# Two decode layers on one core: MLP columns in another order, ninth rows whole on even and odd partitions, and a shorter end of GELU

## The chip, the cores and the metric

The kernel runs on one core of one Trainium2 chip. The metric is the device time of one execution in microseconds (us). All data are 32-bit floats. The core has a matrix engine (TensorE, PE in the profile; its weight loads are PEld), a vector engine (VectorE, DVE), a scalar engine (ScalarE, ACT), GpSimd (POOL) and a queue engine SP that here only issues transfers (DMAs) from device memory (HBM) into the on-chip memory SBUF. SBUF has 128 partitions. TensorE writes its sums into PSUM.

## The reference

There are two sequences (B = 2) with one new position each. One layer is an attention over a cache of 8,192 keys and values per head, 32 heads of 128, and then a gated MLP of width 4,608. The same weights and caches are used in both layers.

```python
def _B_ref(x, w_gate, w_up, w_down):          # the MLP
    g = jnp.einsum("bsd,df->bsf", x, w_gate)   # 576 -> 4608
    u = jnp.einsum("bsd,df->bsf", x, w_up)
    h = _gelu(g) * u                           # tanh form of GELU
    return jnp.einsum("bsf,fd->bsd", h, w_down)

x = A_x
x = x + _A_ref(_layernorm(x), A_k_cache, A_v_cache, A_wq, A_wo)
x = x + _B_ref(_layernorm(x), B_w_gate, B_w_up, B_w_down)
x = x + _A_ref(_layernorm(x), A_k_cache, A_v_cache, A_wq, A_wo)
x = x + _B_ref(_layernorm(x), B_w_gate, B_w_up, B_w_down)
```

## The kernel before

The kernel is written out by hand as `attention(0)`, `mlp(0)`, `attention(1)`, `mlp(1)`. The second attention goes through the heads in reverse order, so that some keys and values that the first left in SBUF are used again.

**Space and the order of transfers.** All weights and caches go through one SBUF tile, `space`, of 50,176 words per partition. A list, `queue`, holds the loads in the order in which they are to be issued. Each time the program has used a piece, `done(key)` frees its words and `pump()` takes as many loads off the list as find room. `Arena` decides where they go: `ring` gives the first layer's MLP pieces four places of 2,304 words by turns; `fit`, used in the second layer's MLP, looks for a free stretch, first behind the last piece given, then from word 0, then behind each live piece. All loads are issued on SP, one after another; an issue waits until the last reader of its words is done. The waits of SP in the trace also show that an issue waits for the landing of the transfer that stands eight places before it.

**Gate and up, first layer** (`split_rows`, `split_middle`, `split_products`). The 4,608 columns are done in two halves h. For one half and one of the two weights, the 576 rows are seen as 64 groups of 9 neighbouring rows. `split_rows` loads rows 2u and 2u+1 of each group (u = 0 to 3) onto the even and the odd partitions, 64 runs of 2,304 words each. The ninth rows of gate and of up share one piece, `split_middle`. Before, the even partitions held the first quarter of columns of the half and the odd ones the second, and beside each other in the partition lay gate and up: eight transfers over both halves of columns. `split_products` multiplies each piece as soon as it has landed: two sides k, four groups c of 288 columns on four quarters of the array (L1097). A filler product (`idle_products`, L586) follows each piece; its result isn't used.

**Gate and up, second layer** (`all_products`, L1113). Pieces are whole: 5, 4 row groups of gate, then 3, 3, 2, 1 of up (`GU[1]`).

**Activation** (`activate`, L1119 to L1135). For each half v: ScalarE multiplies by 1/sigma (L1122), VectorE transposes 32x32 blocks (L1124), and 36 values per partition go through the tanh form of GELU: VectorE (L1127 to L1129), tanh on ScalarE (L1130), VectorE (L1131, L1132), and the result times 0.5 is written twice into `hT`, by VectorE (L1134) and by ScalarE (L1135).

**Down** (`down`, `DOWN`, L1150). `hT` is the stationary operand with 4 columns. Each row of w_down that a partition holds costs 8 matmul instructions of 144 columns (4 column groups, two instructions each). The rows were seen as 4 blocks t of 128 partitions with 9 neighbouring rows each. The first layer took them in pieces of 4 rows, and the four ninth rows as one last piece (two transfers). The second layer took three whole blocks (9 rows, 2,592 KB) and the fourth in pieces of 3, 3, 2, 1 rows. `IDLE` says how much filler stands ahead of each piece. `add_to_x` (L579) adds the sum to x; at the very end x is stored from SP and from ScalarE.

Of the kernel before, what the change touches and what calls it, by code (L numbers as in the profile page):

```python
# [9 lines left out]
F32 = mybir.dt.float32  # L10
AF = mybir.ActivationFunctionType
ALU = mybir.AluOpType
# [3 lines left out]
P = 128  # L16
B = 2
# [3 lines left out]
D = 576  # L21
DF = 4608
# [6 lines left out]
NU = 9  # L29
EQ = 512  # L30
HG = DF // 16
PAD = 6
NT = 4
NI = DF // (NT * P)
# [90 lines left out]
def decode_layers(ctx, tc, x_in, kc, vc, wq, wo, wg, wu, wd, out):  # L125
    nc = tc.nc
# [4 lines left out]
    once = ctx.enter_context(tc.tile_pool(name="once", bufs=1))  # L131
# [7 lines left out]
    for c in range(4):  # L139
        for s in range(2):  # L140
            lo = 32 * c + s * B
# [6 lines left out]
    queue, ready, places = [], {}, {}  # L148

    def pump():  # L150
        while queue and queue[0]():
            queue.pop(0)

    def done(key):
        arena.free(key)
        pump()

    def part_at(at, n):
        return space[:, at:at + n]
# [78 lines left out]
    def weights(key, n, first, transfers):  # L238

        def make():  # L240
            at = arena.ring(key, n) if first is None else arena.fit(key, n, first)
            if at is None:
                return False
            t = ready[key] = part_at(at, n)
            transfers(t)
            return True

        queue.append(make)
# [22 lines left out]
    def split_rows(name, w, h, u):  # L271

        rows = w[:, DF // 2 * h:DF // 2 * (h + 1)].rearrange("(m r) w -> m r w", r=NU)

        def transfers(t):
            for e in range(2):
                nc.sync.dma_start(t[e::2, :], rows[:, 2 * u + e, :])

        weights((name, 0, h, u), DF // 2, None, transfers)

    def split_middle(h):

        def transfers(t):
            for g, w in enumerate((wg, wu)):
                for e in range(2):
                    lo, n = DF // 4 * (2 * h + e), DF // 4
                    nc.sync.dma_start(
                        t[e::2, n * g:n * (g + 1)], w[:, lo:lo + n].rearrange("(m r) w -> m r w", r=NU)[:, NU - 1, :]
                    )

        weights(("gu", 0, h), DF // 2, None, transfers)

    def down(layer, rows):

        (t0, i0), (t1, i1) = rows[0], rows[-1]
        src = wd.rearrange("(t p i) c -> p t i c", t=NT, i=NI)[:, t0:t1 + 1, i0:i1 + 1, :]

        def transfers(t):
            if t0 == t1:
                nc.sync.dma_start(t.rearrange("p (i c) -> p i c", c=D), src[:, 0])  # L300
            else:
                to = t.rearrange("p (t c) -> p t c", c=D)
                for lo, hi in ((0, 3), (3, NT)):
                    nc.sync.dma_start(to[:, lo:hi, :], src[:, lo:hi, 0, :])

        weights(("d", layer, rows[0]), len(rows) * D, whole_at[layer], transfers)

    def products():

# [9 lines left out]
    def out_rows(layer, g):  # L319
# [13 lines left out]
    GU = [[range(0, 5), range(5, NU)], [range(0, 3), range(3, 6), range(6, 8), single[-1]]]  # L333

    DOWN = [
        [[(t, i) for i in range(lo, lo + 4)] for t in range(NT) for lo in (0, 4)] + [[(t, NI - 1) for t in range(NT)]],
        [[(t, i) for i in range(NI)] for t in range(NT - 1)]
        + [[(NT - 1, i) for i in range(lo, hi)] for lo, hi in ((0, 3), (3, 6), (6, 8), (8, 9))],
    ]

    IDLE = [(2, 2, 2, 2, 2, 2, 2, 2, 1), (4, 4, 4, 1)]

    whole_at = (None, 0)
    def groups(layer):
# [76 lines left out]
    def plan_mlp(layer):  # L421
        if layer == 0:
            for h in range(2):
                for u in range(4):
                    split_rows("g", wg, h, u)
                split_middle(h)
                for u in range(4):
                    split_rows("u", wu, h, u)
        else:
            for g, (name, w) in enumerate((("g", wg), ("u", wu))):  # L430
                for us in GU[g]:
                    half_rows((name, layer, us[0]), w, us, 0)
        for rows in DOWN[layer]:
            down(layer, rows)

    plan_first()
    plan_mlp(0)
# [62 lines left out]
    acc = psum1.tile([P, 2, 512], F32, name="acc")  # L500
# [5 lines left out]
    xps = bank[:, 0:CW]  # L506
# [71 lines left out]
    def add_to_x():  # L578
        nc.vector.tensor_add(x, xps, x)  # L579
# [497 lines left out]
    def mlp(layer):  # L1077
        split = layer == 0
        rstd = norm(split)
        if split:  # L1080
            idle_products(2, 1)
        hT = once.tile([P, 2, NI, 2, 2, B], F32, name="hT", tag="xc")

        def window(u, at):

            return xt[:, PAD + 32 * u - at:PAD + 32 * u - at + 4 * B]

        def split_products(h):

            steps = [(("g", layer, h, u), u, 2, (0,)) for u in range(4)] + [(("gu", layer, h), 4, 1, (0, 1))]  # L1090
            steps += [(("u", layer, h, u), u, 2, (1,)) for u in range(4)]
            for key, u, sides, gs in steps:
                w = ready.pop(key).rearrange("p (k c w) -> p k c w", c=4, w=HG)
                for k in range(2):
                    g, e = (k, 0) if u == 4 else (gs[0], k)
                    for c in range(4):
                        nc.tensor.matmul(  # L1097
                            acc[32 * c:32 * c + 4 * B, h, :HG], window(u, 4 * g + 2 * e), w[:, k, c, :],
                            start=(key == steps[0][0] and k == 0), stop=(key == steps[-1][0] and k == 1),
                        )  # L1100
                done(key)
                if key != steps[-1][0]:
                    idle_products(1, None if h else 1)

        def all_products():

            for g, name in enumerate("gu"):
                for us in GU[g]:
                    w = ready.pop((name, layer, us[0])).rearrange("p (u v c w) -> p u v c w", v=2, c=4, w=HG)
                    for u in us:  # L1110
                        for v in range(2):
                            for c in range(4):
                                nc.tensor.matmul(  # L1113
                                    acc[32 * c:32 * c + 4 * B, v, :HG], window(u, 4 * g), w[:, u - us[0], v, c, :],
                                    start=(g == 0 and u == 0), stop=(g == 1 and u == NU - 1),
                                )
                    done((name, layer, us[0]))

        def activate(v):  # L1119

            o = acc[:, v, :HG]
            nc.scalar.activation(o, o, AF.Copy, scale=rstd)  # L1122
            gu = once.tile([P, NI, 32], F32, name="gu", tag="row")
            nc.vector.transpose(gu, o.rearrange("p (m i) -> p i m", i=NI))  # L1124
            g = gu[:, :, 0:4]
            a = once.tile([P, NI, 4], F32, name="ga", tag="part")
            nc.vector.tensor_mul(a, g, g)  # L1127
            nc.vector.tensor_scalar(a, a, 0.044715, 1.0, op0=ALU.mult, op1=ALU.add)
            nc.vector.tensor_mul(a, a, g)  # L1129
            nc.scalar.activation(a, a, AF.Tanh, scale=math.sqrt(2.0 / math.pi))  # L1130
            nc.vector.scalar_tensor_tensor(a, a, 1.0, g, op0=ALU.add, op1=ALU.mult)  # L1131
            nc.vector.tensor_mul(a, a, gu[:, :, 4:8])  # L1132
            a, to = a.rearrange("p i (e b) -> p (i e) b", b=B), hT[:, v].rearrange("p i e s b -> p (i e) s b")
            nc.vector.tensor_scalar_mul(to[:, :, 0, :], a, 0.5)  # L1134
            nc.scalar.mul(to[:, :, 1, :], a, 0.5)  # L1135

        if not split:
            all_products()
        for v in range(2):
            if split:  # L1140
                split_products(v)
            activate(v)
        for n, rows in enumerate(DOWN[layer]):
            if n < len(IDLE[layer]):
                idle_products(IDLE[layer][n], 0)
            w = ready.pop(("d", layer, rows[0])).rearrange("p (i c) -> p i c", c=D)
            for k, (t, i) in enumerate(rows):
                v, e = divmod(t, 2) if split else (t % 2, t // 2)
                for c in range(4):
                    nc.tensor.matmul(  # L1150
                        xps[32 * c:32 * c + 2 * B, :], hT[:, v, i, e, :, :].rearrange("p s b -> p (s b)"),
                        w[:, k, c * CW:(c + 1) * CW],
                        start=(rows is DOWN[layer][0] and k == 0), stop=(t, i) == (NT - 1, NI - 1),
                    )
            done(("d", layer, rows[0]))
        add_to_x()
        if layer == 0:
            idle_products(1)

    attention(0)  # L1160
    mlp(0)
    attention(1)
    mlp(1)
# [29 lines left out]
```

## Time and profile before

| | |
|---|---|
| median of 3 runs | 2684.25 us (2683.34 to 2684.84) |
| the profiled execution | 2683.47 us |
| its span | 2681.7 us |
| TensorE, VectorE, GpSimd, ScalarE busy | 912.3, 2027.3, 1551.8, 166.9 us |
| moved from HBM | 1152.39 MB |
| first layer's MLP in the timeline | about 1,283 to 1,368 us |
| last piece of up lands, last matmul ends | 2,652.99 us, 2,678.36 us |

The span is the time between the first and the last record of the profiled execution; the execution's own time holds 1.8 us more. A timeline row reads: start in us, duration in us, engine, line, operation, out<-in, partitions x elements, count, and in brackets how long the engine stood idle before it and what released it. A row of stretches reads: from:to, its length, busy time (and count) of PE, PEld, DVE, ACT and POOL, then the granted clock of TensorE as a part of full speed, the mean busy share of the 16 transfer engines, and GB/s.

### The profile page before, as it was taken

The page shows a single profiled execution, that of the slowest core. Times are in us where ns is not written, and L with a number is a line of the kernel's source. Part 1 is how long each engine was busy: PE and PEld are TensorE (multiplying, and loading weights), DVE is VectorE, ACT ScalarE, POOL GpSimd, SP SyncE. Part 2 cuts the span into 40 slices and gives each one's busy share as a digit, 9 for nine tenths or more (in the row PEclk, how much of TensorE's full clock was granted, in tenths as well). Part 3 has the DMA queues.
Part 4 walks back from the last instruction along what each step waited for, and adds up shares of the span by engine and source line. Part 5 has one row for each costly group of instructions (what it writes and reads, how often), then busy time and mean ns, then how long its engine had stood idle before and what let it go on. Part 6 is the DMA issues. An engine that isn't in the chain of part 4 may idle for free. (4 is left out here: it accounts for less than half of the span.)

```text
span 2681.7 us, 16126 instructions
## 1 busy us (share of the span) xinstructions
PE 912.3 (34%) x6484; PEld 288.9 (11%) x6484; DVE 2027.3 (76%) x979; ACT 166.9 (6%) x797; POOL 1551.8 (58%) x408
## 2 busy tenths in 40 slices
PE   1323332233233233334663333223323323332346
PEld 0100010010001000111221101001000100010012
DVE  4878888888888888867037878888888888888740
ACT  0000000000000000000026000000000000000000
POOL 2546676667666766744028457666766666676520
PEclk8656655665566566566986665566566556655678
DMA  9999999999999999999999999999999999999998
GB/s 422 437 434 428 435 434 433 431 433 433 434 432 434 430 436 434 428 431 427 417 414 426 436 434 429 434 435 434 431 431 435 432 433 434 433 430 436 430 426 382
DMA packets 31498, 1153.44 MB, mean 430 GB/s; under 512 B 3880, under 2 KB 3904, under 8 KB 5696
## 3 DMA queue, kind: packets, MB, share of 16 engines
q1 hardware_dynamic: 31384, 1152.40, 99.8%
q8 instruction: 51, 0.84, 0.1%
q14 instruction: 23, 0.19, 0.0%
q10 hardware_dynamic: 40, 0.01, 0.0%
HBM read 1152.39 MB, written 0.00 MB: 430 GB/s over the span
## 5 line engine op out<-in xcount | busy, mean ns | idle before, releaser
L767 POOL TENSOR_TENSOR space<-space 128x3072 f32<-128x3072 f32 (+4 forms) x221 | 1127.8, 5103 | 474.8 <-DVE space L738 335.1
L738 DVE TENSOR_TENSOR space<-space,bank 128x6144 f32<-128x6144 f32 (+4 forms) x223 | 1111.8, 4987 | 300.4 <-DMA space<-in_A_k_cache_dram 230.6
L770 DVE TENSOR_REDUCE scores<-space 128x48 f32<-128x3072 f32 (+4 forms) x223 | 569.3, 2553 | 91.9 <-POOL space L767 91.7
L873 POOL TENSOR_TENSOR space<-space 128x2048 f32<-128x2048 f32 x144 | 390.0, 2708 | 385.7 <-DVE space L870 362.3
L899 PE MATMUL acc<-space,prz 128*8 128x512 f32 x3328 | 509.6, 776 | 206.6 <-DMA space<-in_A_v_cache_dram 202.5
L653 PE MATMUL bank<-qsb,pick 4*64 4x128 f32 (+1 forms) x256 | 45.4, 432 | 850.9 <-DVE space L738 843.3
L870 DVE TENSOR_TENSOR space<-space,bank 128x4096 f32<-128x4096 f32 x48 | 212.2, 4420 | 1.6
L899 PEld LDWEIGHTS acc<-space,prz 128*8 128x8 f32 x3328 | 98.7, 107 | 559.4 <-issue 356.8
L819 ACT ACTIVATE nbs<-bank 128x2 f32<-128x2 f32 (+1 forms) x68 | 11.6, 171 | 1812.4 <-PE bank L804 1782.8
L921 PE MATMUL bank<-of,wide 128*32 128x2 f32 x512 | 40.9, 202 | 237.9 <-DVE wide L914 237.9
L653 PEld LDWEIGHTS bank<-qsb,pick 4*64 4x64 f32 (+1 forms) x256 | 20.3, 200 | 872.3 <-DVE space L738 855.5
L796 PE MATMUL bank<-ident,m 128*1 128x128 f32 x68 | 21.7, 319 | 242.5 <-DVE m L794 242.3
L575 POOL TENSOR_TENSOR rstd<-ve,mhalf 128x1 f32<-128x1 f32 x4 | 2.2, 550 | 176.0 <-DVE ve L573 176.0
L878 PE MATMUL acc<-space,owner 128*8 128x512 f32 x96 | 89.9, 1039 | 0.0
L1124 DVE STREAM_TRANSPOSE gu<-acc 128x288 f32<-128x288 f32 x4 | 1.9, 483 | 93.2 <-ACT acc L1122 93.2
L921 PEld LDWEIGHTS bank<-of,wide 128*32 128x32 f32 x512 | 35.7, 154 | 326.1 <-DVE wide L914 324.9
L835 PE MATMUL bank<-sums,unit 128*128 128x2 f32 x120 | 35.2, 363 | 86.9 <-ACT prz L827 86.9
L913 DVE TENSOR_TENSOR acc<-acc,diag 128x512 f32<-128x512 f32 x64 | 43.5, 679 | 27.6 <-PE acc L899 27.6
L940 ACT ACTIVATE oT<-bank,rinv 32x8 f32<-32x8 f32 x110 | 28.5, 259 | 381.5 <-PE bank L921 380.8
L827 ACT ACTIVATE prz<-scores,nbs 64x128 f32<-64x128 f32 (+1 forms) x128 | 50.7, 396 | 17.2 <-POOL prz L817 14.4
L760 ACT ACTIVATE space<-space 128x128 f32<-128x128 f32 x164 | 48.4, 296 | 19.4 <-DVE space L738 16.5
L804 PE MATMUL bank<-m,unit 1*128 1x2 f32 (+1 forms) x136 | 38.5, 350 | 25.6 <-DVE m L802 25.6
(100 smaller groups left out, 519.0 us busy)
## 6 DMA issues: line engine op xcount, KB each, us to landing
space<-in_A_k_cache_dram SPq DMA_DIRECT2D x6, 4096.0 KB
space<-in_A_v_cache_dram SPq DMA_DIRECT2D x5, 4096.0 KB
space<-in_A_wo_dram SPq DMA_DIRECT2D x15, 1152.0 KB
space<-in_B_w_gate_dram SPq DMA_DIRECT2D x16, 576.0 KB
space<-in_B_w_up_dram SPq DMA_DIRECT2D x16, 576.0 KB
space<-in_B_w_down_dram SPq DMA_DIRECT2D x8, 1152.0 KB
space<-in_A_v_cache_dram SPq DMA_DIRECT2D x4, 2048.0 KB
space<-in_A_wq_dram SPq DMA_DIRECT2D x16, 512.0 KB
```

The costliest lines, as they stand in the source:

```text
L653: nc.tensor.matmul(qb[n][to, :], pick[32 * c:32 * c + 4, r:r + 1].to_broadcast([4, P // it.heads]), qsb[32 * c:32 * c + 4, (h % 4) * DH:(h ...
L738: nc.vector.tensor_tensor(out=u[:, :r, :], in0=t[:, :r, :], in1=qb[n].unsqueeze(1).to_broadcast([P, r, DH]), op=ALU.mult)
L760: nc.scalar.activation(u[:, j, :], u[:, j, :], AF.Copy, accum_out=S[n][:, base(n, k) + j:base(n, k) + j + 1])
L767: nc.gpsimd.tensor_tensor(out=half, in0=half, in1=u[:, :r, DH // 2:], op=ALU.add)
L770: nc.vector.tensor_reduce(out=S[n][:, base(n, k):base(n, k) + own_rows(n, k, m)], in_=prod.pop((n, k)), axis=AX.X, op=ALU.add)
L827: nc.scalar.activation(pr[at, lo:].rearrange("p (g e) -> p g e", e=4)[:, 0:it.rows // 2:2, :], s[at, :it.rows].rearrange("p (g r) -> p g r ...
L870: nc.vector.tensor_tensor(out=t, in0=t, in1=share.unsqueeze(2).to_broadcast([P, rows, DH]), op=ALU.mult)
L873: nc.gpsimd.tensor_tensor(out=t[:, :rows], in0=t[:, :rows], in1=t[:, rows:2 * rows], op=ALU.add)
L878: nc.tensor.matmul(accumulator(n)[0:8, :], owner.rearrange("p a e -> p (a e)"), part_at(arena.live[key, lo][0], 4 * DH), start=False, stop ...
L899: nc.tensor.matmul(accumulator(n)[32 * c:32 * c + 8, :], pr[:, at:at + 8], t[g // 4][:, g % 4 * 4:g % 4 * 4 + 4, :].rearrange("p j d -> p ...
L913: nc.vector.tensor_tensor(out=q, in0=q, in1=diag.unsqueeze(2).to_broadcast([P, 4, DH]), op=ALU.mult)
L921: nc.tensor.matmul(po[lo:lo + 32, i, :], t[:, i::GH], of, start=True, stop=True)
```

## The change

It changes which column of the 4,608 stands where. The columns are now numbered so that partition p of `down` holds 18 neighbouring rows of w_down (2 blocks h of 128 x 18 instead of 4 of 128 x 9). The gate and up products pick their columns to fit: the moving operand is read in runs of 9 words out of 18. The ninth rows of gate go whole onto the even partitions and those of up onto the odd ones, in 4 transfers instead of 8. Down's last piece in the first layer has runs of two rows instead of one; in the second layer down has five pieces (18, 12, 3, 2, 1 rows) instead of seven, and the fillers ahead of them become (8, 8, 1) instead of (4, 4, 4, 1). In the activation, g*u*0.5 is formed beside tanh, and two combined operations on VectorE write `hT`; ScalarE's last step goes.

```diff
@@ split_middle
-                for e in range(2):
-                    lo, n = DF // 4 * (2 * h + e), DF // 4
-                    nc.sync.dma_start(
-                        t[e::2, n * g:n * (g + 1)], w[:, lo:lo + n].rearrange("(m r) w -> m r w", r=NU)[:, NU - 1, :]
-                    )
+                rows = w[:, DF // 2 * h:DF // 2 * (h + 1)].rearrange("(m r) w -> m r w", r=NU)
+                nc.sync.dma_start(t[g::2, :], rows[:, NU - 1, :])
@@ down
-        src = wd.rearrange("(t p i) c -> p t i c", t=NT, i=NI)[:, t0:t1 + 1, i0:i1 + 1, :]
+        src = wd.rearrange("(h p r) c -> p h (r c)", h=2, r=2 * NI)
...
+            for h, lo, hi in piece:
+                nc.sync.dma_start(t[:, at:at + (hi - lo) * D], src[:, h, lo * D:hi * D])
+                at += (hi - lo) * D
@@ DOWN, IDLE
-        [[(t, i) for i in range(lo, lo + 4)] for t in range(NT) for lo in (0, 4)] + [[(t, NI - 1) for t in range(NT)]],
-        [[(t, i) for i in range(NI)] for t in range(NT - 1)]
-        + [[(NT - 1, i) for i in range(lo, hi)] for lo, hi in ((0, 3), (3, 6), (6, 8), (8, 9))],
+        [[(h, lo, lo + 4)] for h in range(2) for lo in range(0, 16, 4)] + [[(h, 16, 18) for h in range(2)]],
+        [[(0, 0, 18)]] + [[(1, lo, hi)] for lo, hi in ((0, 12), (12, 15), (15, 17), (17, 18))],
-    IDLE = [(2, 2, 2, 2, 2, 2, 2, 2, 1), (4, 4, 4, 1)]
+    IDLE = [(2, 2, 2, 2, 2, 2, 2, 2, 1), (8, 8, 1)]
@@ split_products
-                w = ready.pop(key).rearrange("p (k c w) -> p k c w", c=4, w=HG)
+                w = ready.pop(key).rearrange("p (c m k i) -> p k c m i", c=4, k=2, i=NI)
...
-                            acc[32 * c:32 * c + 4 * B, h, :HG], window(u, 4 * g + 2 * e), w[:, k, c, :],
+                            acc[32 * c:32 * c + 4 * B, h, :HG], window(u, 4 * k + 2 * g), w[:, k, c],
@@ all_products
-                    w = ready.pop((name, layer, us[0])).rearrange("p (u v c w) -> p u v c w", v=2, c=4, w=HG)
+                    w = ready.pop((name, layer, us[0])).rearrange("p (u c m v i) -> p u v c m i", m=32, v=2, c=4, i=NI)
@@ activate
-            nc.vector.scalar_tensor_tensor(a, a, 1.0, g, op0=ALU.add, op1=ALU.mult)
-            nc.vector.tensor_mul(a, a, gu[:, :, 4:8])
-            a, to = a.rearrange("p i (e b) -> p (i e) b", b=B), hT[:, v].rearrange("p i e s b -> p (i e) s b")
-            nc.vector.tensor_scalar_mul(to[:, :, 0, :], a, 0.5)
-            nc.scalar.mul(to[:, :, 1, :], a, 0.5)
+            nc.vector.tensor_mul(of_by, g, u)
+            nc.vector.tensor_scalar_mul(by, by, 0.5)
...
+            for s in range(2):
+                nc.vector.scalar_tensor_tensor(to[:, :, s, :], a, 1.0, by, op0=ALU.add, op1=ALU.mult)
@@ mlp, down's products
-                v, e = divmod(t, 2) if split else (t % 2, t // 2)
+                v, e = (h, r // NI) if split else (r // NI, h)
```

More of the change, by code (lines that the diff above doesn't have):

```diff
@@ L284, in transfers, with down @@
             for g, w in enumerate((wg, wu)):
-                for e in range(2):
-                    lo, n = DF // 4 * (2 * h + e), DF // 4
-                    nc.sync.dma_start(
-                        t[e::2, n * g:n * (g + 1)], w[:, lo:lo + n].rearrange("(m r) w -> m r w", r=NU)[:, NU - 1, :]
-                    )
+                rows = w[:, DF // 2 * h:DF // 2 * (h + 1)].rearrange("(m r) w -> m r w", r=NU)
+                nc.sync.dma_start(t[g::2, :], rows[:, NU - 1, :])
         weights(("gu", 0, h), DF // 2, None, transfers)
-    def down(layer, rows):
-        (t0, i0), (t1, i1) = rows[0], rows[-1]
-        src = wd.rearrange("(t p i) c -> p t i c", t=NT, i=NI)[:, t0:t1 + 1, i0:i1 + 1, :]
+    def down(layer, piece):
+        src = wd.rearrange("(h p r) c -> p h (r c)", h=2, r=2 * NI)
         def transfers(t):
[L299 to L306, printed above, removed]
+            at = 0
+            for h, lo, hi in piece:
+                nc.sync.dma_start(t[:, at:at + (hi - lo) * D], src[:, h, lo * D:hi * D])
+                at += (hi - lo) * D
+        weights(("d", layer, piece[0]), sum(hi - lo for _, lo, hi in piece) * D, whole_at[layer], transfers)
     def products():
@@ L432, in plan_mlp @@
                     half_rows((name, layer, us[0]), w, us, 0)
-        for rows in DOWN[layer]:
-            down(layer, rows)
+        for piece in DOWN[layer]:
+            down(layer, piece)
     plan_first()
@@ L1088, in split_products @@
         def split_products(h):
-            steps = [(("g", layer, h, u), u, 2, (0,)) for u in range(4)] + [(("gu", layer, h), 4, 1, (0, 1))]
-            steps += [(("u", layer, h, u), u, 2, (1,)) for u in range(4)]
-            for key, u, sides, gs in steps:
-                w = ready.pop(key).rearrange("p (k c w) -> p k c w", c=4, w=HG)
+            steps = [(("g", layer, h, u), u, 0) for u in range(4)] + [(("gu", layer, h), 4, 0)]
+            steps += [(("u", layer, h, u), u, 1) for u in range(4)]
+            for key, u, g in steps:
+                w = ready.pop(key).rearrange("p (c m k i) -> p k c m i", c=4, k=2, i=NI)
                 for k in range(2):
-                    g, e = (k, 0) if u == 4 else (gs[0], k)
                     for c in range(4):
                         nc.tensor.matmul(
-                            acc[32 * c:32 * c + 4 * B, h, :HG], window(u, 4 * g + 2 * e), w[:, k, c, :],
+                            acc[32 * c:32 * c + 4 * B, h, :HG], window(u, 4 * k + 2 * g), w[:, k, c],
                             start=(key == steps[0][0] and k == 0), stop=(key == steps[-1][0] and k == 1),
@@ L1113, in all_products @@
                                 nc.tensor.matmul(
-                                    acc[32 * c:32 * c + 4 * B, v, :HG], window(u, 4 * g), w[:, u - us[0], v, c, :],
+                                    acc[32 * c:32 * c + 4 * B, v, :HG], window(u, 4 * g), w[:, u - us[0], v, c],
                                     start=(g == 0 and u == 0), stop=(g == 1 and u == NU - 1),
@@ L1124, in activate @@
             nc.vector.transpose(gu, o.rearrange("p (m i) -> p i m", i=NI))
-            g = gu[:, :, 0:4]
-            a = once.tile([P, NI, 4], F32, name="ga", tag="part")
-            nc.vector.tensor_mul(a, g, g)
+            order = "p i (e g b) -> p g i e b" if split else "p i (g e b) -> p g i e b"
+            sides = gu[:, :, 0:8].rearrange(order, g=2, b=B)
+            g, u = sides[:, 0], sides[:, 1]
+            ga = once.tile([P, 2, NI * 2 * B], F32, name="ga", tag="part")
+            a, by = ga[:, 0], ga[:, 1]
+            of_a, of_by = [t.rearrange("p (i e b) -> p i e b", e=2, b=B) for t in (a, by)]
+            nc.vector.tensor_mul(of_a, g, g)
             nc.vector.tensor_scalar(a, a, 0.044715, 1.0, op0=ALU.mult, op1=ALU.add)
-            nc.vector.tensor_mul(a, a, g)
+            nc.vector.tensor_mul(of_a, of_a, g)
             nc.scalar.activation(a, a, AF.Tanh, scale=math.sqrt(2.0 / math.pi))
-            nc.vector.scalar_tensor_tensor(a, a, 1.0, g, op0=ALU.add, op1=ALU.mult)
-            nc.vector.tensor_mul(a, a, gu[:, :, 4:8])
-            a, to = a.rearrange("p i (e b) -> p (i e) b", b=B), hT[:, v].rearrange("p i e s b -> p (i e) s b")
-            nc.vector.tensor_scalar_mul(to[:, :, 0, :], a, 0.5)
-            nc.scalar.mul(to[:, :, 1, :], a, 0.5)
+            nc.vector.tensor_mul(of_by, g, u)
+            nc.vector.tensor_scalar_mul(by, by, 0.5)
+            a, by = [t.rearrange("p (k b) -> p k b", b=B) for t in (a, by)]
+            to = hT[:, v].rearrange("p i e s b -> p (i e) s b")
+            for s in range(2):
+                nc.vector.scalar_tensor_tensor(to[:, :, s, :], a, 1.0, by, op0=ALU.add, op1=ALU.mult)
         if not split:
@@ L1142, in mlp @@
             activate(v)
-        for n, rows in enumerate(DOWN[layer]):
+        for n, piece in enumerate(DOWN[layer]):
             if n < len(IDLE[layer]):
                 idle_products(IDLE[layer][n], 0)
-            w = ready.pop(("d", layer, rows[0])).rearrange("p (i c) -> p i c", c=D)
-            for k, (t, i) in enumerate(rows):
-                v, e = divmod(t, 2) if split else (t % 2, t // 2)
+            w = ready.pop(("d", layer, piece[0])).rearrange("p (i c) -> p i c", c=D)
+            for k, (h, r) in enumerate((h, r) for h, lo, hi in piece for r in range(lo, hi)):
+                v, e = (h, r // NI) if split else (r // NI, h)
                 for c in range(4):
                     nc.tensor.matmul(
-                        xps[32 * c:32 * c + 2 * B, :], hT[:, v, i, e, :, :].rearrange("p s b -> p (s b)"),
+                        xps[32 * c:32 * c + 2 * B, :], hT[:, v, r % NI, e, :, :].rearrange("p s b -> p (s b)"),
                         w[:, k, c * CW:(c + 1) * CW],
-                        start=(rows is DOWN[layer][0] and k == 0), stop=(t, i) == (NT - 1, NI - 1),
+                        start=(n == 0 and k == 0), stop=(h, r) == (1, 2 * NI - 1),
                     )
-            done(("d", layer, rows[0]))
+            done(("d", layer, piece[0]))
         add_to_x()
```

## The prediction

> **What bounds the kernel now.** I read the page's span and queue rows first, then its slices, then the chain of waits, then the timeline and the stretches around the two places the diff touches: the first layer's MLP (1,283 to 1,368 us) and the kernel's last 65 us.
>
> ```profile
> span 2681.7 us, 16126 instructions
> ...
> DMA  9999999999999999999999999999999999999998
> GB/s 422 437 434 428 435 434 433 431 433 433 434 432 434 430 436 434 428 431 427 417 414 426 436 434 429 434 435 434 431 431 435 432 433 434 433 430 436 430 426 382
> ...
> q1 hardware_dynamic: 31384, 1152.40, 99.8%
> ...
> HBM read 1152.39 MB, written 0.00 MB: 430 GB/s over the span
> ```
>
> One queue carries 1,152.4 MB and its packets fill 99.8% of the 16 transfer engines' time. No compute engine is near that. So a change gains or loses time in three ways only: the same bytes move faster or slower, the queue runs empty, or the work behind the last landing gets longer. The change moves the same bytes. The two slices of the first MLP (417, 414) stand 3% under the rest: all that small pieces cost there is some 4 us of two 67 us slices.
>
> The end of the kernel, from the last piece of up (TensorE rows, then the issues of down on SP):
>
> ```profile
> 2652.99 1.16 PE L1113 MATMUL acc<-space,xt 128*8 128x288 f32 x16 [0.67 <-DMA space<-in_B_w_up_dram]
> ...
> 2657.86 2.72 PE L586 MATMUL acc<-ident 128*4 128x512 f32 x3 [3.72 <-DVE gu L1124]
> 2659.53 0.66 PE L1150 MATMUL bank<-space,hT 128*4 128x144 f32 x6
> ...
> 2668.07 1.88 PE L586 MATMUL acc<-ident 128*4 128x512 f32 x4
> 2671.50 2.39 PE L1150 MATMUL bank<-space,hT 128*4 128x144 f32 x72 [1.55 <-DMA space<-in_B_w_down_dram]
> 2673.70 0.38 PE L586 MATMUL acc<-ident 128*4 128x256 f32 x1
> ...
> 2675.77 0.92 PE L1150 MATMUL bank<-space,hT 128*4 128x144 f32 x24 [0.74 <-DMA space<-in_B_w_down_dram]
> 2677.18 1.14 PE L1150 MATMUL bank<-space,hT 128*4 128x144 f32 x24 [0.49 <-DMA space<-in_B_w_down_dram]
> ```
> ```profile
> 2677.89 0.11 PEld L1150 LDWEIGHTS bank<-space,hT 128*4 128x4 f32 x8 [0.35 <-DMA space<-in_B_w_down_dram]
> 2678.39 0.31 DVE L579 TENSOR_TENSOR x<-bank,x 128x144 f32<-128x144 f32 x1 [18.90 <-PE bank L1150]
> ```
> ```profile
> 2620.54 0.33 SPq L300 DMA_DIRECT2D space<-in_B_w_down_dram  x1
> 2623.17 0.33 SPq L300 DMA_DIRECT2D space<-in_B_w_down_dram  x1
> 2629.28 0.33 SPq L300 DMA_DIRECT2D space<-in_B_w_down_dram  x1
> ...
> 2650.21 0.33 SPq L300 DMA_DIRECT2D space<-in_B_w_down_dram  x1
> ```
>
> Each row of w_down costs 8 matmul instructions. Down's pieces land at 2671.50 (the third of nine rows), 2675.77, 2677.18 and 2677.89, and TensorE waits for each: the end is set by transfers, with 0.5 us behind the last (2677.89 to 2678.39), then the sum into x and the store of x.
>
> **The change, part by part.**
>
> *Transfers, first layer.* The ninth gate and up rows: 8 transfers of 64 runs of 4,608 bytes become 4 of 64 runs of 9,216. Down's last piece: 512 runs of 2,304 bytes become 256 of 4,608. The other pieces of down keep 9,216-byte runs and only stand twice as far apart in memory.
>
> ```profile
> 1300.00:1304.00 4.00, 2.86 (x40) 0.87 (x32) 0.00 (x0) 0.00 (x0) 0.00 (x0) 1.00 1.02 412
> 1344.00:1354.00 10.00, 8.06 (x138) 3.73 (x136) 0.77 (x4) 0.47 (x2) 0.00 (x0) 1.00 1.01 422
> 2618.00:2645.00 27.00, 15.72 (x196) 5.76 (x192) 0.00 (x0) 0.00 (x0) 0.00 (x0) 0.82 0.99 425
> ```
>
> The last number of each row is GB/s: the stretch in which the ninth rows land, the one in which 9,216-byte runs of down land, and the one in which gate and up of the second layer land in runs of 27 to 46 KB. 3.5 MB going from 412 to 422 is 8.5 to 8.3 us, a gain of 0.2 us. That is one end. The other: the wider spacing brings down's 9.4 MB from 422 to 412, 22.3 to 22.9 us, 0.6 lost. I take 0.1 us gained, near no change, since nothing in the rows ties the rate to spacing.
>
> *Transfers, second layer.* Seven pieces of down become five: 18 rows, 12, 3, 2, 1. Before, three pieces of nine rows (7.96 MB) land between 2652.99 and 2671.50: 430 GB/s, the whole kernel's mean, so longer runs have nothing to gain there. I take 0.1 us for the two transfers less (ends 0 and 0.3, which is 1% of the 25 us).
>
> *Where the larger pieces go.* The space is handed out in program order, so this can be worked out from the code. The 18-row piece (10,368 words) takes words 32,256 to 42,623: exactly what the first two nine-row pieces took. It can be issued when the second of those could, at 2623.17 and no longer half at 2620.54. The 12-row piece takes 11,520 to 18,431 and like the third piece before (2629.28) waits for the sixth gate row; the others end at the same words as before. Covering work: until 2652.99 the queue still moves gate and up, 30 us. If that cover were gone, the price would be the 2.6 us between the two issues. Behind the waiting issue on SP stand only down's other pieces and the store of x. The issues also wait for a transfer eight places earlier:
>
> ```profile
> SPq L300 <- DMA space<-in_B_w_up_dram: 18.8, 3, 7.8
> ```
>
> With two transfers fewer, the last one no longer waits for the third up piece (2650.21) but for the first. Nothing there is late. Cost: nothing.
>
> *TensorE at the end.* This is the term I can name a cost for. The 18-row piece lands at 2652.99 plus 5.31 MB at 430 GB/s = 2665.3 us; its 144 matmul instructions go at 2.39/72 = 33 ns (4.8 us) to 2670.1. Then 8 filler products instead of 4: four started 0.43 us apart in the 1.88 us from 2668.07, so 3.5 us, to 2673.6. The 12-row piece lands at 2665.3 + 8.2 (3.54 MB at 430 GB/s) = 2673.5, so they just fit. Then 96 instructions, 3.2 us, to 2676.8; two fillers of half width, 0.4, to 2677.2; three rows (landed 2675.8) 0.85, to 2678.0; two rows 0.55; one row 0.3: the last starts near 2678.6 and ends 0.2 later, near 2678.9 to 2679.1 where before it ends at 2678.36. Late next is TensorE itself, no more the transfer. I take +0.65 us. The low end is 0: the two filler groups and the 12 rows' start hang on the 18 rows' landing, and 0.65 us earlier there would undo it. The high end hangs on the clock:
>
> ```profile
> 2628.30 5.76 PE L1113 MATMUL acc<-space,xt 128*8 128x288 f32 x64 [3.72 <-DMA space<-in_B_w_gate_dram]
> ```
> ```profile
> 2628.00:2630.00 2.00, 1.70 (x17) 0.66 (x21) 0.00 (x0) 0.00 (x0) 0.00 (x0) 0.63 1.03 442
> ...
> 2670.00:2672.00 2.00, 0.50 (x18) 0.44 (x22) 0.00 (x0) 0.00 (x0) 0.00 (x0) 1.00 0.95 381
> ```
>
> After a pause of 3.72 us the granted clock (third number from the end) was down to 0.63 in the mean of 2 us; after one of 1.55 us, before 2671.50, it was still 1.00. The change leaves TensorE a pause from about 2663.2 (eight fillers from 2657.86, some five at 2.72/3 = 0.9 us and three at 0.43) to 2665.3, 2.1 us, between the two. Were the clock halved there, the first 3 us of the 144 instructions do the work of 1.5 us and the end moves with them and the fillers: +1.5 to +3 more.
>
> *GELU's end.*
>
> ```profile
> 2655.97 0.23 ACT L1130 ACTIVATE ga<-ga 128x36 f32<-128x36 f32 x1 [1.23 <-DVE ga L1129]
> ...
> 2656.70 0.23 ACT L1135 ACTIVATE hT<-ga 128x36 f32<-128x36 f32 x1 [0.49 <-DVE ga L1132]
> 2656.84 0.46 ACT L1122 ACTIVATE acc<-acc,rstd 128x288 f32<-128x288 f32 x1
> ```
>
> From tanh's start to the end of hT is 0.96 us before. After, VectorE does g*u and the half beside tanh, then two combined operations, all four at 0.23 us from start to start as here,
>
> ```profile
> 2656.24 0.20 DVE L1131 SCALAR_TENSOR_TENSOR ga<-ga,gu 128x36 f32<-128x36 f32 x1 [0.30 <-ACT ga L1130]
> 2656.47 0.20 DVE L1132 TENSOR_TENSOR ga<-ga,gu 128x36 f32<-128x36 f32 x1
> ```
>
> some 0.9 us in all. One ScalarE instruction goes, so the second half's scaling (2656.84) can start some 0.5 us earlier. Worth about 0.6 us to hT, and nothing to the kernel: before, the down products started at 2659.53, after they can't start before 2665.3, when the 18 rows land. In the first layer TensorE waits for a landing at every piece. Gain taken: nothing (ends 0 and 0).
>
> *Order of columns.* The gate and up products now read their moving operand from SBUF in runs of 9 words with gaps of 9, where before it was 288 words in a row. No row of this trace shows such a read. The first layer's rows give the slack:
>
> ```profile
> 1324.58 1.16 PE L1097 MATMUL acc<-space,xt 128*8 128x288 f32 x16 [1.30 <-DMA space<-in_B_w_gate_dram]
> 1325.55 0.60 PE L586 MATMUL bank<-ident 128*4 128x128 f32 x4
> 1327.39 1.16 PE L1097 MATMUL acc<-space,xt 128*8 128x288 f32 x16 [1.24 <-DMA space<-in_B_w_gate_dram]
> ```
>
> A piece lands every 2.81 us and asks for 1.16 us of products and 0.60 of fillers. Up to 1.9 times the product time, nothing is felt. The nearest rows are the fillers with 128x512: they read 128 words four times over, four runs in place of one, at 0.43 us for 512 columns (0.84 ns a column on one quarter of the array), against 1.16/16 = 72 ns for 288 columns with four quarters at work (4 x 72/288 = 1.0 ns a column): runs cost nothing visible. I take a factor of 1.0, with ends 1 and 3. In the second layer the last up piece (16 instructions, 1.16 us) is followed by 6 us in which hT waits for the 18 rows, so that even a factor of 3 (2.3 us more) is hidden there.
>
> [...]
>
> *Sum.* The profiled execution took 2683.47 us for its span of 2681.7. 2683.47 - 0.1 - 0.1 + 0.65 = 2683.9. The median of the runs shown, 2684.25, is 0.78 above that execution, so the forecast against the median is 2684.7 us: no change that can be told. About 0.2% (5.4 us) is what a measurement of this kernel can tell.
>
> **Rivals.**
>
> *Slower: the broken-up moving operand slows the first layer's products.* With a factor f, each of 17 steps lags by 1.16 f + 0.60 - 2.81 us. Four ring places absorb about three landings (8.4 us) less one piece's own products, some 5 us, before the queue runs dry. f = 2.5: 17 x 0.69 = 11.7, less 5.5 is 6 us; from here it decides. f = 3: 21.6 - 5 = 17 us, about 2701 us. For it: no row shows such reads. Against it: the fillers' four runs, and 36 bytes in a row in each run.
>
> *Slower, but not by what can be told: the granted clock falls at the end.* +2.4 us on the forecast (the middle of 1.5 to 3), 2687. For it the row at 2628, against it the row at 2670, and the new pause is nearer to the shorter one.
>
> *Faster: the transfers gain.* If all 14 MB of changed pieces went at the kernel's best slice, 437 GB/s in place of 412 (the worst stretch above), the gain is 34.0 - 32.0 = 2 us; 2682. To pass 5.4 us it would have to lift the neighbours too. Against: the queue is 99.8% busy with the same bytes.
>
> *It doesn't do what it says:* no transfer gain and no shorter GELU in effect is the forecast + 0.2 us, inside it.
>
> **How the numbers follow.** Forecast, with the clock rival and small transfer gains, all within 0.2%: 0.83 (0.60 for the forecast's own 2683 to 2686, 0.13 for the clock, 0.10 for the gain). Broken-up operand from f = 2.5: 0.11; another slowing that I can't place (down's wider spacing in memory among it): 0.03. Faster by over 0.2%: 0.03. The range goes from 2682.0 (the gain) to 2689.5 (the clock's +3 with a run's spread of 1.5): it leaves out the 0.14 above and the 0.03 below.
>
> **What would show it.** Right: queue 1 at 99.8% and 430 GB/s; the first layer's products still 16 instructions in 1.16 us; 72-instruction groups of down replaced by 144 and 96, the latter starting near 2673.6; the last down matmul 0.4 to 0.8 us later behind the last landing; a transfer count lower by 6. Wrong: products of 16 instructions at 2.5 us or more, a DMA share under 0.95 between 1,290 and 1,370, or a last group at half clock.

## The result and the profile after

The changed kernel takes 2761.01 us (median of 5 runs, 2760.25 to 2762.66) against 2684.25 us before (median of 5 as well): a ratio of 1.029, with a 95% interval of 1.0278 to 1.0301. It is 77 us slower. The forecast was 2684.7 us, no change, so it was wrong, and the time lies far outside the forecast's range.

The page of the changed kernel, with the rows that answer to those shown of before:

```profile
span 2759.2 us, 16120 instructions
...
DMA  9999999999999999998469999999999999999998
GB/s 426 431 435 431 434 434 432 435 432 434 432 433 434 432 433 433 430 430 367 154 268 421 435 436 429 438 428 437 429 436 431 435 432 433 434 432 433 434 425 372
...
q1 hardware_dynamic: 30520, 1152.40, 97.3%
```

The bytes are the same; the queue has fallen from 99.8% to 97.3% busy, and all of the fall lies in three slices (367, 154, 268 GB/s): the first layer's MLP. There the queue runs empty. Twenty microseconds of that stretch, before and after (same columns as in the prediction: the last three numbers are granted clock, transfer share and GB/s):

```profile
1300.00:1320.00 20.00, 12.45 (x137) 3.90 (x130) 1.53 (x7) 0.73 (x3) 0.00 (x0) 0.91 1.02 422
```
```profile
1300.00:1320.00 20.00, 8.18 (x54) 2.21 (x54) 0.00 (x0) 0.00 (x0) 0.00 (x0) 0.50 0.36 124
```

TensorE is no busier than before, it is idler (8.18 for 12.45 us), and at half clock (0.50 for 0.91). So it isn't the new bound. The rows of the first gate products of the changed kernel (L1089 was L1097, L579 the fillers' L586):

```profile
1301.88 2.11 PE L1089 MATMUL acc<-space,xt 128*8 128x288 f32 x16 [8.33 <-DMA space<-in_B_w_gate_dram]
1303.75 1.06 PE L579 MATMUL acc<-ident 128*4 128x256 f32 x2
1309.49 2.11 PE L1089 MATMUL acc<-space,xt 128*8 128x288 f32 x16 [4.68 <-DMA space<-in_B_w_up_dram]
1311.36 1.06 PE L579 MATMUL acc<-ident 128*4 128x256 f32 x2
1317.68 2.11 PE L1089 MATMUL acc<-space,xt 128*8 128x288 f32 x16 [5.26 <-DMA space<-in_B_w_up_dram]
...
1411.84 2.11 PE L1089 MATMUL acc<-space,xt 128*8 128x288 f32 x16 [5.05 <-DMA space<-in_B_w_up_dram]
```

The bracket is what to read. The second and third products use pieces of *gate*, but what ends their wait is the landing of rows of *up*, which stand three places further down the list: the ninth rows' piece, whose second load is up's, and then up's first piece. And SP, in the same stretch, waits far longer for these products to free a place (first row: before; then the changed kernel: time in all, times, longest):

```profile
SPq L277 <- PE acc L1097: 10.4, 8, 3.0
```
```profile
SPq L277 <- PE acc L1089: 79.7, 12, 7.0
SPq L286 <- PE acc L1089: 18.3, 2, 11.6
```
```profile
1304.04 0.47 SPq L286 DMA_DIRECT2D space<-in_B_w_gate_dram  x1
1304.56 0.59 SPq L286 DMA_DIRECT2D space<-in_B_w_up_dram  x1
...
1311.65 0.47 SPq L277 DMA_DIRECT2D space<-in_B_w_up_dram  x1
```

The two wait for each other. A product waits until the last load issued so far has landed; its end frees one place; SP issues one more piece (1311.65, just after the fillers begin at 1311.36); the next product waits until that one has landed (1317.68). One piece at a time goes through a ring of four. The step from 1309.49 to 1317.68 is 2.11 us of products and 6.03 us from the issue at 1311.65 to the landing. Half clock has a share in it: by the 1.23 us that such a group takes at full clock (measured below), some 0.9 us a step, an estimate.

The list of the built program's instructions, with the semaphores that each waits for, shows that the waits were put there when the program was built (transfers count on eight semaphores by turns, DMAHW0 to 7; here the first products of the first three gate pieces):

```
before   L1097 MATMUL acc<-space,xt 8x288 [waits DMAHW2,DMAHW1,DVE]
         L1097 MATMUL acc<-space,xt 8x288 [waits DMAHW4,DMAHW3]
         L1097 MATMUL acc<-space,xt 8x288 [waits DMAHW6,DMAHW5]
after    L1089 MATMUL acc<-space,xt 8x288 [waits DMAHW4,DMAHW3,DMAHW5,DMAHW2,DMAHW6,DMAHW1,DMAHW7,DMAHW0,DVE]
         L1089 MATMUL acc<-space,xt 8x288 [waits DMAHW2,DMAHW1]
         L1089 MATMUL acc<-space,xt 8x288 [waits DMAHW4,DMAHW3]
```

Before, each product waits for the two loads of its own piece. After, the first waits for all eight, and the second for the ninth rows' two loads, which were issued last by then. The words that it reads overlap with none of the other pieces. Both sides have gaps now: the read along the partition (9 words of 18) and the loads across the partitions (every second one). The hypothesis to test: the program's tracking of the big tile can't tell such a read and such a load apart, and takes them as overlapping.

The time adds up. Before, 17 steps from 1294.27 to 1341.27 us (the starts of the first and the last product group of L1097) are 2.76 us each.

```profile
1294.27 1.16 PE L1097 MATMUL acc<-space,xt 128*8 128x288 f32 x16 [0.48 <-DVE ve L573]
...
1341.27 1.16 PE L1097 MATMUL acc<-space,xt 128*8 128x288 f32 x16 [1.12 <-DMA space<-in_B_w_up_dram]
```

After, the first starts 7.6 us late, and 14 steps from 1301.88 to 1411.84 are 7.85 us each: 14 x 5.09 = 71.3. The last three pieces have then all landed and go 1.6 us faster than before. 7.6 + 71.3 - 1.6 = 77.3 us, and the spans differ by 2759.2 - 2681.7 = 77.5.

### The profile page after: what moved, and what is told of

Its sections match the earlier page's. It is cut to its first block, busy times and chain, and to the rows that moved or that the text cites. A ratio compares the mean times of both kernels' runs of the same rounds, so it can differ in the third digit from the quotient of the medians.

```text
span 2759.2 us, 16120 instructions
## 1 busy us (share of the span) xinstructions
PE 932.4 (34%) x6488; PEld 294.2 (11%) x6488; DVE 2027.4 (73%) x983; ACT 166.1 (6%) x793; POOL 1552.7 (56%) x408
## 3 DMA queue, kind: packets, MB, share of 16 engines
q1 hardware_dynamic: 30520, 1152.40, 97.3%
## 5 line engine op out<-in xcount | busy, mean ns | idle before, releaser
L646 PEld LDWEIGHTS bank<-qsb,pick 4*64 4x64 f32 (+1 forms) x256 | 20.4, 200 | 869.6 <-DVE space L731 852.8
L1089 PE MATMUL acc<-space,xt 128*8 128x288 f32 x288 | 37.1, 648 | 78.1 <-DMA space<-in_B_w_up_dram 49.4
```

The lines of the kernel that those rows point to most:

```text
L646: nc.tensor.matmul(qb[n][to, :], pick[32 * c:32 * c + 4, r:r + 1].to_broadcast([4, P // it.heads]), qsb[32 * c:32 * c + 4, (h % 4) * DH:(h ...
```

## The experiments

Three explanations stood against each other. A: the waits, as above. B: TensorE reads the broken-up operand slowly (the rival of the prediction). C: something else of the change, such as the ninth rows' transfers or down's wider spacing.

**The read alone, in the kernel before.**

```diff
-                w = ready.pop(key).rearrange("p (k c w) -> p k c w", c=4, w=HG)
+                w = ready.pop(key).rearrange("p (c m k i) -> p k c m i", c=4, k=2, i=NI)
```

> The kernel before with one edit: the first layer's gate and up products read their pieces in runs of 9 words out of 18; transfers, ninth rows, GELU and down stay as before (each product gets other columns than it should, so the MLP of the first layer is computed with permuted columns). Theory A (waits: the read in runs makes the program wait for every load issued so far, since it can't be told apart from loads onto every second partition): about 2,760 us, the transfer share falls to 0.4 in the first MLP, a step of 16 products takes about 8 us. Rival B (TensorE reads the broken-up operand slowly): also slow, but TensorE's busy time grows by as much as the span. Rival C (the other order of transfers, the ninth rows or down's wider spacing): 2,684 us.

Measured: 2762.26 us, ratio 1.0293 (1.0263 to 1.0323). The read alone brings the whole loss; C falls as its cause.

**The change with whole reads in the first layer.**

```diff
-                w = ready.pop(key).rearrange("p (c m k i) -> p k c m i", c=4, k=2, i=NI)
+                w = ready.pop(key).rearrange("p (k c w) -> p k c w", c=4, w=HG)
```

> The changed kernel with the first layer's gate and up products reading 288 words in a row again (columns permuted there); all else is the change. A and B: the 76 us in the first MLP go, about 2,684 to 2,687 us, what is left being the second layer's end. C: 2,760 us.

Measured: 2684.62 us, ratio 1.0005 (0.9994 to 1.0016). All the rest of the change together, the second layer's reads in runs of 9 among it, can't be told from nothing.

**One broken read per piece.** The kernel before, its 16 products unchanged, with one small product more:

```diff
+                runs = w.rearrange("p k c w -> p (k c w)").rearrange("p (c m k i) -> p k c m i", c=4, k=2, i=NI)
+                nc.tensor.matmul(turned[0:4 * B, 0:8 * NI], window(u, 0), runs[:, 0, 0, 0:8], start=True, stop=True)
```

> The kernel before, whose products read 288 words in a row, with one small extra product per piece of the first layer (72 columns in runs of 9, into a place that nothing reads; one product of two instructions beside 16). A: the one read draws all the waits, about 2,760 us. B: 18 products of some 0.1 us, all beside transfers: 2,684 us.

Measured: 2765.61 us, ratio 1.0306 (1.0276 to 1.0336). In its timeline the small product (72 columns) is the one that waits; the 288-column products behind it read whole rows:

```profile
1310.03 0.28 PE L1095 MATMUL bank<-space,xt 128*8 128x72 f32 x1 [5.16 <-DMA space<-in_B_w_up_dram]
1310.04 0.66 PE L1099 MATMUL acc<-space,xt 128*8 128x288 f32 x3
```

A read of some 0.3 us can't cost 5 us a step by its own rate. B falls, and the wait is what costs. The lists of the built programs agree: here and with the read alone the first product in runs of 9 waits for all eight semaphores, and here the extra waits stand on the 72-column products; with whole reads, and in the kernels with other loads below, each product waits for the loads of its own piece and for no other load.

**The broken read, with loads onto neighbouring partitions.** The change, but with pieces of 128 neighbouring rows (the last 64 of gate and of up in one piece, a half of the partitions each):

```diff
-        rows = w[:, DF // 2 * h:DF // 2 * (h + 1)].rearrange("(m r) w -> m r w", r=NU)
-            for e in range(2):
-                nc.sync.dma_start(t[e::2, :], rows[:, 2 * u + e, :])
+        rows = w[P * u:P * (u + 1), DF // 2 * h:DF // 2 * (h + 1)]
+            nc.sync.dma_start(t, rows)
...
+                nc.sync.dma_start(t[HALF * g:HALF * (g + 1), :], rows)
```

> The changed kernel, with reads in runs of 9, but each gate and up piece of the first layer is loaded as 128 neighbouring rows in one transfer onto partitions 0 to 127 (the last 64 rows onto one half of the partitions each) instead of every second partition; the rows so meet the wrong inputs. A: no load is mistaken any more, about 2,684 to 2,687 us. B: the read is as broken up as in the change, 2,760 us.

Measured: 2694.85 us, ratio 1.0041 (1.0021 to 1.0061). 66 of the 77 us are gone though every read is still broken, so it takes both sides. But 11 us stay, which no theory had. The stretches of this kernel say where:

```profile
1300.00:1310.00 10.00, 4.22 (x36) 0.99 (x28) 0.00 (x0) 0.00 (x0) 0.00 (x0) 0.83 1.00 218
1310.00:1320.00 10.00, 5.53 (x66) 1.85 (x70) 0.00 (x0) 0.00 (x0) 0.00 (x0) 1.00 1.00 415
...
1330.00:1340.00 10.00, 4.29 (x40) 1.63 (x40) 0.00 (x0) 0.00 (x0) 0.00 (x0) 0.84 1.01 219
```

In the two stretches where the ninth rows land the transfer engines are fully busy (1.00 and 1.01) and move half as much (218 and 219 GB/s; 415 in the row between). Those are the loads onto one closed half of the partitions, of my own making here. Two of them hold 1.18 MB together, and 10 us at 218 GB/s move 2.18 MB, so the piece ahead of them is slowed with them: its products start at 1306.51 here and at 1302.14 in the kernel that follows. The next kernel loads the ninth rows' piece, too, onto all 128 at once:

```diff
-                nc.sync.dma_start(t[HALF * g:HALF * (g + 1), :], rows)
+            nc.sync.dma_start(t, wg[7 * HALF:, DF // 2 * h:DF // 2 * (h + 1)])
```

> As the kernel with plain loads, but the ninth rows' piece too is one transfer of 128 neighbouring rows (gate's last 128; up's ninth rows are left out). If the 11 us that the plain loads still cost come from the two transfers onto one half of the partitions (two stretches of 10 us at 218 GB/s where 415 is usual, 4.7 us each), 2,684 to 2,686 us. If they come from the reads in runs of 9 (16 products in 1.23 us where 1.16 before), 2,694 us again.

Measured: 2684.17 us, ratio 1.0002 (0.9991 to 1.0012). The 11 us came with the half-partition loads. And this kernel gives the price of the broken read by itself, since nothing waits falsely and the clock is full (1.00 from 1,280 to 1,340 us):

```profile
1302.14 1.23 PE L1086 MATMUL acc<-space,xt 128*8 128x288 f32 x16 [1.15 <-DMA space<-in_B_w_gate_dram]
```
```profile
L1086 PE MATMUL acc<-space,xt x288: 422/422/437, 1294.3 to 1341.9; 128*8 128x288 f32 x144
```
```profile
L1097 PE MATMUL acc<-space,xt x288: 402/406/687, 1294.3 to 1342.0; 128*8 128x288 f32 x144
```

The second and third rows are one line's instructions of this kernel and of the kernel before: least, median and most ns. A group of 16 products takes 1.23 us for 1.16, a factor of 1.06; one instruction 422 ns for 406, a factor of 1.04.

**The change in full, with the first layer loaded as the second is.**

```diff
-            for h in range(2):
-                for u in range(4):
-                    split_rows("g", wg, h, u)
-                split_middle(h)
-                for u in range(4):
-                    split_rows("u", wu, h, u)
+            for name, w in (("g", wg), ("u", wu)):
+                for us in single:
+                    half_rows((name, layer, us[0]), w, us, None)
...
-        split = layer == 0
+        split = False
```

> The whole change with a right result, but the first layer's gate and up are loaded as the second layer's are: 9 pieces of 128 half rows each, one transfer per piece onto all partitions, both halves of columns finished together. Theory A: no load is mistaken, 2,684 to 2,687 us; the reads in runs of 9 stay. If something else of the change costs time in the first layer (the wider spacing of down, its last piece), it shows here as more than 2,687.

Measured: 2684.69 us, ratio 1.0004 (0.9995 to 1.0013). So the order of columns that the change wants can be had without the 77 us, if the loads fill all partitions. It gains nothing that can be told either: the queue was full before (99.8%), and the same bytes still have to pass it.

**The broken read in one half of the columns only** (9 of 18 steps).

```diff
+                if h == 0:
+                    w = w.rearrange("p (c m k i) -> p k c m i", c=4, k=2, i=NI)
+                else:
+                    w = w.rearrange("p (k c w) -> p k c w", c=4, w=HG)
```

> The change with the read in runs of 9 only in the first half of the first layer's columns (9 of 18 steps); the second half reads 288 words in a row (permuted columns). Theory A with a price of some 5 us a step: half of 77 us, about 2,723 us. If the cost were paid once (an emptied queue that has to be filled again), about 2,755 or near 2,690.

Measured: 2732.26 us, ratio 1.0181 (1.016 to 1.0201): 48 us, not the 38 that I expected of a half. The price is per step, but not even. The nine products start from 1301.88 to 1365.14:

```profile
1301.88 2.11 PE L1093 MATMUL acc<-space,xt 128*8 128x288 f32 x16 [7.61 <-DMA space<-in_B_w_gate_dram]
...
1365.14 2.11 PE L1093 MATMUL acc<-space,xt 128*8 128x288 f32 x16 [4.94 <-DMA space<-in_B_w_gate_dram]
```

Eight steps of 7.9 us, each 5.1 above 2.76, make 41, and the first wait adds 7.6: 49. In the whole change only 14 of 17 steps pay, since the last three pieces have been issued before the last false wait ends. So the first half of the columns holds the late start and eight paying steps, and the second half only six.

**Fillers at the end.** Whole reads in the first layer, and the second layer's fillers moved ahead:

```diff
-    IDLE = [(2, 2, 2, 2, 2, 2, 2, 2, 1), (8, 8, 1)]
+    IDLE = [(2, 2, 2, 2, 2, 2, 2, 2, 1), (14, 0, 0)]
```

> The changed kernel with whole reads in the first layer (as the second experiment), and the fillers ahead of down in the second layer 14, 0, 0 instead of 8, 8, 1. If fillers between the pieces hold back the end: the last matmul ends about 0.5 us behind the last landing, some 24.9 us after the last up products begin, where with 8, 8, 1 it was 25.4; the granted clock is 1.0 when the 18 rows land. On the median 0 to -1 us, which can't be told.

Measured: 2684.89 us, ratio 1.0003 (0.9993 to 1.0012), and the expectation of the end was wrong. Timeline and stretches of this kernel:

```profile
2665.19 4.59 PE L1147 MATMUL bank<-space,hT 128*4 128x144 f32 x144 [1.12 <-DMA space<-in_B_w_down_dram]
2673.40 6.26 PE L1147 MATMUL bank<-space,hT 128*4 128x144 f32 x144 [3.62 <-DMA space<-in_B_w_down_dram]
```
```profile
2675.00:2677.00 2.00, 2.00 (x40) 1.41 (x36) 0.00 (x0) 0.00 (x0) 0.00 (x0) 0.50 0.27 107
```

The clock was kept for the 18 rows (1.00 from 2,663 to 2,667 us), but without fillers TensorE then stands still for 3.62 us and does part of the other 18 rows at half clock. From the last up products (2651.97) to the last matmul's end (2679.66) it took 27.7 us, not 24.9. With 8 fillers between the pieces, in the kernel with whole reads, it took 25.4 (rows below). That is one trace of each; the medians, 2684.89 and 2684.62 us, can't tell the two apart.

## Why the prediction was wrong, point by point

- **What bounds the kernel: right**, and the reason why the loss is one to one. The queue was 99.8% busy before, and the time that the steps lost came back in full: 77.3 us over the steps, 77.5 us in the span.
- **Order of columns: the step that failed.** It was costed at nothing. It weighed only the rate at which TensorE reads runs of 9 words, between 1 and 3, took 1.0, and the factor is 1.06; its nearest row, the filler's four runs of 128 words, is far from 32 runs of 9. It never asked for whom the new read waits. In the place of nothing the runs showed 7.6 us ahead of the first step and 5.09 us in each of 14, less 1.6 us at the end: the 77 us. "Where the larger pieces go" followed which words each load takes, and the text took it for granted that a product waits for its own piece and a load for the last reader of its own words. The loads still do; with a read and a load that both have gaps the products don't. The kernel with one small extra product shows that one such read is enough; the one with whole reads and the one with loads onto all partitions show that both sides are needed. Why the tracking takes the two as overlapping stays open; the waits in the list and the times are what is shown. Of the prediction's own signs of being wrong, the one that came is the transfer share under 0.95 in the first MLP (0.36).
- **The slower rival: right line, wrong mechanism.** It put the slowing on the broken-up operand in the first layer, with 0.11, and asked for a product time 2.5 times as long. The product groups do take 2.11 us where 1.16 stood, but at half clock: in the kernel before, a group that met half clock took as long (the row below), and with nothing waiting falsely it is 1.23. Of what the prediction set against it, the 36 bytes in a row in each run had no row behind them; the runs put the price of such reads at 422 ns for 406 of one instruction.

```profile
1307.85 2.11 PE L1097 MATMUL acc<-space,xt 128*8 128x288 f32 x16 [1.72 <-DMA space<-in_B_w_up_dram]
```

- **Transfers, GELU's end: right as far as can be told.** The change with whole reads stands at 1.0005 (0.9994 to 1.0016). GELU's end did shorten: from tanh's start to the end of `hT` it is 0.70 us in the changed kernel, where it was 0.96. It bought nothing, as said: down's products still begin with the landing of the 18 rows.

```profile
2732.15 0.23 ACT L1126 ACTIVATE ga<-ga 128x36 f32<-128x36 f32 x1 [1.23 <-DVE ga L1125]
```
```profile
2732.55 0.30 DVE L1132 SCALAR_TENSOR_TENSOR hT<-ga 128x36 f32<-128x36 f32 x2
```

- **TensorE at the end: the sum held as long as the clock did.** The changed kernel and the second experiment, from the last up products on:

```profile
2729.08 1.25 PE L1105 MATMUL acc<-space,xt 128*8 128x288 f32 x16 [0.59 <-DMA space<-in_B_w_up_dram]
...
2741.26 6.27 PE L1147 MATMUL bank<-space,hT 128*4 128x144 f32 x144 [2.65 <-DMA space<-in_B_w_down_dram]
...
2754.14 1.63 PE L1147 MATMUL bank<-space,hT 128*4 128x144 f32 x42
```
```profile
2652.64 1.25 PE L1105 MATMUL acc<-space,xt 128*8 128x288 f32 x16 [0.59 <-DMA space<-in_B_w_up_dram]
...
2664.83 4.59 PE L1147 MATMUL bank<-space,hT 128*4 128x144 f32 x144 [1.42 <-DMA space<-in_B_w_down_dram]
...
2673.04 3.12 PE L1147 MATMUL bank<-space,hT 128*4 128x144 f32 x96 [0.20 <-DMA space<-in_B_w_down_dram]
...
2676.41 1.63 PE L1147 MATMUL bank<-space,hT 128*4 128x144 f32 x42
```

Before, it was 25.4 us from 2652.99 to 2678.36. With the pause at 1.42 us the 144 instructions took 4.59 us (I had 4.8) and the end 25.4 us again, where I forecast 0.65 more: the 12 rows started 20.4 us after the last up products (2673.04), where I had 20.6, and from there to the end it took 5.0 us, where I had about 5.4. The term was too large. With the pause at 2.65 us they took 6.27, with a granted clock of 0.60 in the mean of the first 2 us, and the end 26.7 us, 1.3 more: the clock rival, at about half its price.

## What to carry to other kernels

Before costing a new access pattern by its speed, ask which waits the program will put on it: a pattern with gaps, on a large tile into which many loads with gaps go, can be taken for a reader of all of them, as here, where the first product waited for all eight semaphores. The sign in this profile was a consumer whose wait was ended by a load that it didn't use (4.68 us ahead of 1309.49), with the queue running empty (a transfer share of 0.36) and TensorE busy for 8.18 of 20 us; the waits in the list of the built program tell it before any run. When such a read is wanted, load onto neighbouring partitions, which took the false waits away here (2694.85 us for 2761.01), and onto all 128 at once, which kept the rate (2684.17 us, with 417 GB/s from 1,300 to 1,320 us).

## What the runs showed of the hardware

- Loads of 64 rows onto every second partition moved at 422 GB/s (the kernel before, 1,300 to 1,320 us). With loads of as many rows onto 64 neighbouring partitions under way, the queue moved half of it: 218 and 219 GB/s with the transfer engines 100% busy (the kernel with loads onto neighbouring partitions, 1,300 to 1,310 and 1,330 to 1,340 us). No run shows why.
- A moving operand in runs of 36 bytes with gaps as long cost 4% by the single instruction (422 for 406 ns) and 6% by the group of 16 (1.23 for 1.16 us; 1.25 in the second layer, in the row at 2729.08).
- TensorE's granted clock outlived pauses of 1.12 and 1.42 us in the runs above and fell after, or in, pauses of 2.65 and 3.62 us. The length of a pause did not decide it alone: in the kernel before it fell about a pause of 1.72 us (the row at 1307.85; 0.64 in the mean of 1,307 to 1,309 us, then 0.50), and in the kernel with loads onto neighbouring partitions it held over one of 1.76 us (the group at 1299.64 took 1.23 us).
